# Attention and feed-forward on one core: transposes between second-product matmuls, a Prelu leaky step and a new schedule

## The chip, the cores and the metric

The kernel runs on one core of one Trainium2 chip. The metric is the device time of one execution in microseconds (us). The kernel before took 1224.76 us, the median of three runs (1224.69 to 1225.83).

## What is computed

Attention over 8 batches of 8 heads, 576 tokens of 64 numbers each, with a causal mask in blocks of 64 tokens; then a feed-forward part with a leaky step over all 4608 tokens:

```python
scores = np.where(block_i >= block_j, 0.125 * q @ k.T, -1e9)      # blocks of 64 tokens
attn = exp(scores - max); attn /= sum + 1e-9
x = (attn @ v), heads side by side                                 # 4608 x 512
h = x @ w_in                                                       # 512 -> 2048
out = np.maximum(0.01 * h, h) @ w_out                              # 2048 -> 512
```

All is float32. The weights come as 64-bit floats and are turned into float32 on the chip.

## The kernel before, in words

**Products in two halves.** Most products use the faster 32-bit format (fp32r). A float32 operand is split into a high part, a rounded copy, and a low part, the rest (`gh` and `gl`, `xh` and `xl`, `kh` and `kl`, `pth` and `ptl`), and a product is the sum of two or three matmuls. In batch 0 the scores of some heads and all values are plain float32 matmuls (L408, L539).

**Work.** The attention of batch 0 is done in two passes, `lo` (the first 320 tokens) and `hi` (the other 256) of each of its 8 heads; the 56 heads of batches 1 to 7 are `full`. A full head has five tiles of rows: tile 0 with 64 rows, tiles 1 to 4 with 128, each as wide as its mask allows (64, 192, 320, 448 and 576 columns). Its steps: scale and split q and k (L196 to L206, L393); scores of tiles 3, 0, 1, 2 into the two banks `p_s`, later of tile 4 (L411); mask (L420), row maximum (L427), exponential and row sum (L436), reciprocal (L450, L451) and normalising (L464 to L466, by GpSimd, VectorE or ScalarE); 15 transposes in groups of 4, 4, 5 and 2 into the two banks `p_t` (L487); the copies `pth` and `ptl`; 10 matmuls with the values (L542); the sums into `xr` (L528, L564).

**Feed-forward.** The tokens go in 18 chunks of 256. A chunk has 8 units of 256 of the 2048 inner columns. A unit has two runs of 12 matmuls of 256 columns into `p_h` (L630, the first product), then the leaky step into `g`: 0.01 h by ScalarE (or VectorE), from PSUM, and a maximum on VectorE, also from PSUM (L637). Then come `gh` and `gl`, and two runs of 6 matmuls of 512 columns into `p_o` (L648, the second product).

**Weights.** 64 pieces are loaded and converted by shifts and masks on VectorE (L319, L323); every other piece takes its sign by a third VectorE instruction (L328), the rest by a ScalarE sign (L332) and a GpSimd product (L333).

**Order.** No engine's order is written by hand. Each step is given to `Plan` with its buffers, an engine (or several to choose from), a price in ns, and a rank; a list schedule over the five engines then takes, on each engine that is free, the ready step of the lowest rank, and the instructions are issued in that order. The ranks come from the constants at the top of the file (RL to AHEAD). `HOLD` is how much longer a second choice of engine must wait than the first. Matmuls are priced at `max(109, n / 2.4 + 2.5)`, transposes at 109. While nothing else is ready early on, PE repeats a fill matmul (L701).

Of the kernel before, what the change touches and what calls it, by code (L numbers as in the profile page):

```python
# [32 lines left out]
# Ranks of the steps, in heads: inputs, preparation, wide tile, transposes, values, sums into x, normalising.  # L33
RL = 2.876
RP = 0.212
RB = 0.6
RT = 1.102
RV = 1.747
RX = 1.545
RN = -0.217  # L40
# Ranks of the feed-forward part and of the weights.
LEAD = 1.791
LAG = 1.995
RS = 1.48
RG = -0.41
OFF1 = 6
SL1 = 12.747
AHEAD = 0.041
# DMA latency; the fills that keep TensorE's clock up until the feed-forward part starts.
LAT = 1550  # L50
FILL = 235
FILLTO = 12


class Plan:
# [3 lines left out]
    HOLD = 816.955  # L59
# [14 lines left out]
    def add(self, choices, rank, reads=(), writes=(), lag=0):  # L74
        i = len(self.ops)
        deps = set()
        for k in reads:
            if k in self.writer:
                deps.add(self.writer[k])
        for k in writes:  # L80
            if k in self.writer:
                deps.add(self.writer[k])
            deps.update(self.readers.get(k, ()))
        for k in reads:
            self.readers.setdefault(k, []).append(i)
        for k in writes:
            self.writer[k] = i
            self.readers[k] = []
        deps.discard(i)
        self.ops.append((choices, rank, deps, lag))  # L90

    def run(self):
        n = total = len(self.ops)
        left = [len(o[2]) for o in self.ops]
        after = [[] for _ in range(n)]
# [3 lines left out]
        ends = [None] * n  # L99
# [3 lines left out]
        order, now, moved = [], 0, 0  # L103

        def offer(i):
            for k, (e, _, _) in enumerate(self.ops[i][0]):
                at = max([0] + [ends[d][1] + self.SYNC.get((ends[d][0], e), 0) for d in self.ops[i][2]])
                heapq.heappush(waiting, (at + k * self.HOLD, i, k))

        for i in range(n):  # L110
            if not left[i]:
                offer(i)
        while len(order) < n:
            while waiting and waiting[0][0] <= now:
                _, i, k = heapq.heappop(waiting)
                heapq.heappush(ready[self.ops[i][0][k][0]], (self.ops[i][1], i, k))
            for e, q in ready.items():
                while q and ends[q[0][1]]:
                    heapq.heappop(q)
                if q and free[e] <= now:  # L120
                    _, i, k = heapq.heappop(q)
                    choices, _, _, lag = self.ops[i]
                    _, cost, fn = choices[k]
                    if e == "PE" and now < 8000:
                        cost *= 2
                    free[e] = now + cost
                    if lag:
                        moved = max(moved, free[e] + 650) + lag
                    ends[i] = (e, moved + LAT if lag else free[e])
                    order.append(fn)  # L130
                    for j in after[i]:
                        left[j] -= 1
                        if not left[j]:
                            offer(j)
            if self.fill and free["PE"] <= now and now > self.fill[2]:
                if any(self.ops[i][0][0][0] == "PE" and self.ops[i][1] < self.fill[3] and not ends[i] for i in range(total)):
                    order.append(self.fill[1])
                    free["PE"] = now + self.fill[0] * (1 if now > 8000 else 2)
                    n += 1
                else:  # L140
                    self.fill = None
            times = [free[e] for e, q in ready.items() if (q or (e == "PE" and self.fill)) and free[e] > now]
            if waiting:
                times.append(waiting[0][0])
            if len(order) < n:
                now = max(now, min(times))
        for fn in order:
            fn()


def mm(n):
    return max(109, n / 2.4 + 2.5)


def product(n, plain):
    return max(109, n / 0.6) if plain else 2 * mm(n)
# [14 lines left out]
def pool2(n):  # L171
    return n * 2.35 + 25


def pool1(n):
    return n * 0.83 + 245
# [3 lines left out]
def attention_ffn(ctx: ExitStack, tc: tile.TileContext, qk: bass.AP, v: bass.AP, w_in: bass.AP, w_out: bass.AP, out: bass.AP):  # L180
# [13 lines left out]
    def copying(n, dst, src, sb=True, by=None, first="ACT", fast=True):  # L194
# [6 lines left out]
        both = [("ACT", act(n, sb), one), ("DVE", dve(n, sb and fast), two)]  # L201
        return both if first == "ACT" else both[::-1]

    def subtracting(n, dst, one, two, first="DVE"):
        both = [
            ("DVE", dve(n), lambda: nc.vector.tensor_sub(dst(), one(), two())),  # L206
# [26 lines left out]
    def rows(y, pool):  # L233
        prow[y] = [fixed([P, pw[t]], F32, f"prow{y}_{t}", None, pool) for t in range(NT)]
        for t in range(NT):
            nc.gpsimd.memset(prow[y][t][:, 0:BLK] if t == 0 else prow[y][t][:, kw[t] : pw[t]], 0.0)
# [45 lines left out]
    def weight_piece(num, rank, f, out_side, c0):  # L282
# [28 lines left out]
        if src.dtype != F32:  # L311

            def load():
# [5 lines left out]
                [("DVE", dve(w, True), lambda: nc.vector.tensor_single_scalar(bits(), bits(), 3, op=ALU.logical_shift_left))],  # L319
# [3 lines left out]
                [("DVE", dve(w), lambda: nc.vector.scalar_tensor_tensor(  # L323
# [3 lines left out]
            if num % SIGNS:  # L327
                add([("DVE", dve(w), lambda: nc.vector.scalar_tensor_tensor(  # L328
# [14 lines left out]
    def attention(i):  # L343
# [44 lines left out]
        else:  # L388
# [4 lines left out]
                [("DVE", dve(qe - qa), lambda: nc.vector.scalar_tensor_tensor(  # L393
# [10 lines left out]
        def scores(tiles):  # L404
            for t, ap, k0, k1 in tiles:
                cols = slice(q0[t], q0[t] + qn[t])
                if plain_s:
                    nc.tensor.matmul(ap, qkt[:rows, 0, cols], qkt[:rows, 1, k0:k1], start=True, stop=True)  # L408
                    continue
                for c, kk in enumerate((kh[z], kl[z])):  # L410
                    nc.tensor.matmul(ap, qs[z][:, cols], kk[:, k0:k1], start=c == 0, stop=c == 1)  # L411

        def softmax(tiles, mms, masks, r):
            banks = sorted({(sk, bk) for _, _, bk in tiles for bk in bk})
            cost = sum(product(k1 - k0, plain_s) for _, _, k0, k1 in mms)
            add([("PE", cost, lambda: scores(mms))], r, qkd, banks)
# [7 lines left out]
            for t, ap, bk in tiles:  # L424
# [3 lines left out]
                        nm[z][: qn[t], t : t + 1], ap, axis=AX.X if flat else AX.XY, op=ALU.max, negate=True  # L428
# [3 lines left out]
            def exponent(t, ap, flat):  # L432
                o = row(t, qn[t], pc[t], kw[t])
                if not flat:
                    o = o.rearrange("p (a k) -> p a k", a=2)
                nc.scalar.activation(  # L436
                    o, ap, AF.Exp, bias=nm[z][: qn[t], t : t + 1], scale=1.0, accum_out=sums[z][: qn[t], t : t + 1]
# [19 lines left out]
        def normalising(t, rr):  # L457
            by = rec[z][:rr, t : t + 1]

            def p():  # L460
# [4 lines left out]
                ("DVE", dve(kw[t], True), lambda: nc.vector.tensor_scalar_mul(p(), p(), by)),  # L465
# [4 lines left out]
        tiles = [(t, scored(k)[: qn[t], c : c + kw[t]], (k,)) for t, k, c in lay]  # L470
        softmax(
            tiles, [(t, ap, 0, kw[t]) for t, ap, _ in tiles],
            [ap[0:64, kw[t] - 64 : kw[t]] for t, ap, _ in tiles if t], r0,
        )
        if kind != "lo":
            softmax(
                [(4, p_s[:, :, 0:288], (0, 1))],
                [(4, p_s[:, 0, 0:288], 0, 288), (4, p_s[:, 1, 0:288], 288, 576)],
                [p_s[0:64, 1, 224:288]], r0 + RB,
            )  # L480
        for base, c0, w, items in tgroups[kind]:
            x = bank()

            def transposes(x=x, items=items):
                for t, j, c in items:
                    r = qn[t]
                    nc.tensor.transpose(p_t[x][:, c : c + r], row(t, r, j * P, P), ident[:r, :r])  # L487

            add([("PE", 109 * len(items), transposes)], r0 + RT, [k for t in sorted({a for a, _, _ in items}) for k in pkeys(t)], [("t", x)])
# [7 lines left out]
            def lo(base=base, w=w):  # L497
# [4 lines left out]
                subtracting(w, lo, lambda src=src: src, lambda hi=hi: hi)[:1],  # L502
# [34 lines left out]
        def passes(dst, j, cols, start, stop):  # L537
            if plain_v:
                nc.tensor.matmul(dst[0:64], vf[z][:, j], ptf[:, cols], start=start, stop=stop)  # L539
                return  # L540
            for k, pp in enumerate((pth, later["ptl"])):
                nc.tensor.matmul(dst, vs[z][:, j, :], pp[:, cols], start=start and k == 0, stop=stop and k == 1)  # L542

        def outer():
            c, w = ends[kind]
            passes(p_t[x0][:, :w], 0, slice(c, c + w), True, True)

        def values():
            last = spans[kind][-1][0]
            for j, a, e, c in spans[kind]:  # L550
                passes(p_t[x1][:, c : c + e - a], j, slice(a, e), j == 1, j == last)

        if kind in ends:
            add([("PE", product(ends[kind][1], plain_v), outer)], rv, ptd + [vkey], [("t", x0)])
        cost = sum(product(e - a, plain_v) for _, a, e, _ in spans[kind])
        add([("PE", cost, values)], rv, ptd + [vkey], [("t", x1)])
# [13 lines left out]
    def bank():  # L570
# [7 lines left out]
    }  # L578
    tgroups = {
# [16 lines left out]
        "full": [(1, 0, 512, 0), (2, 512, 960, 64), (3, 960, 1280, 192), (4, 1408, 1600, 320)],  # L596
# [23 lines left out]
    def ffn1(c, u, rank):  # L620
# [3 lines left out]
        for i in range(2):  # L624
            f = 2 * u + i

            def go(i=i, f=f):
                terms = [(w, x, d) for d in range(ND) for w, x in ((wih, xh), (wih, xl), (wil, xh))]
                for k, (w, x, d) in enumerate(terms):
                    nc.tensor.matmul(  # L630
                        hh[:, i, :], w[:, d, f * P : (f + 1) * P], x[:, d, :], start=k == 0, stop=k == len(terms) - 1
                    )
# [99 lines left out]
```

## Time and profile before

One execution was profiled; the span from its first to its last instruction is 1226.6 us, 1.84 us above the median of the three runs.

| engine | busy, us | share of the span |
|---|---|---|
| PE (matmuls) | 1188.9 | 97% |
| PEld (weight loads, beside PE) | 1056.9 | 86% |
| DVE (VectorE) | 785.2 | 64% |
| ACT (ScalarE) | 655.1 | 53% |
| POOL (GpSimd) | 476.0 | 39% |

A line of a group names the source line, the engine, the operation, what is written from what, the shapes and the count; then busy us and mean ns, and the idle time in front of it with what ended it. A line of the timeline begins with the start and the duration. A matmul's duration contains its way through the pipeline, so neighbouring matmuls overlap, and what one costs is read from the distance of starts.

### The profile page before, as it was taken

To read this page: it belongs to the slowest core of one execution; us is meant where nothing else is said; L and a number is where in the kernel's file an instruction comes from. 1 tells how busy PE (TensorE), PEld (TensorE's weight loads), DVE (VectorE), ACT (ScalarE), POOL (GpSimd) and SP (SyncE) were. 2 spreads that over 40 slices of the span, in tenths; PEclk is the share of its full clock that TensorE was granted. 3 is DMA by queue.
4 is the path that set the end of the run, shared out by engine and by line. 5 is a ranking of instruction groups with operands and counts; after the bars stand their busy time and mean duration, and the time that the engine had idled before them with its cause. 6 is when DMAs were issued, how large, how long until landed. Compare 5 with 4: busy or idle time off the path is not lost.

```text
span 1226.6 us, 21217 instructions
## 1 busy us (share of the span) xinstructions
PE 1188.9 (97%) x7718; PEld 1056.9 (86%) x7718; DVE 785.2 (64%) x1904; ACT 655.1 (53%) x1635; POOL 476.0 (39%) x569
## 2 busy tenths in 40 slices
PE   8888889899999999999999999999999999999998
PEld 6676678789999999999899999999999999999997
DVE  7989999888766767664454566767676766421110
ACT  6767755556555555554455455555555655422221
POOL 5687753334433334333333333433333333222222
PEclk9889999999999999999999999999999999999999
DMA  5555421221111211111111021112111110000000
GB/s 169 180 161 174 164 73 55 70 63 61 48 68 50 68 50 68 50 45 49 43 50 43 25 68 50 67 51 68 50 66 39 56 50 20 10 18 1 18 18 18
DMA packets 40233, 76.44 MB, mean 62 GB/s; under 512 B 4032, under 2 KB 23360, under 8 KB 40128
## 3 DMA queue, kind: packets, MB, share of 16 engines
q1 hardware_dynamic: 40128, 75.09, 19.1%
q8 instruction: 60, 0.98, 0.3%
q14 instruction: 45, 0.37, 0.1%
HBM read 65.63 MB, written 9.44 MB: 61 GB/s over the span
## 4 chain that ended last, share of the span: by engine, by line
PE 80%; DVE 14%; issue 2%; ACT 1%; DMA 1%; POOL 0%; SPq 0%; DVEq 0%; ACTq 0%; POOLq 0%
PE p_h L630 30%; PE p_o L648 29%; PE p_t L487 8%; PE p_t L542 6%; PE p_s L411 6%; DVE prow L465 2%; DVE val L323 2%; DVE nm L427 2%; DVE val L319 1%; DVE qs L393 1%; DVE val L328 1%; DVE kl L206 1%; DVE ptl L206 1%; DVE g L637 1%; DVE p_s L420 0%
## 5 line engine op out<-in xcount | busy, mean ns | idle before, releaser
L207 POOL TENSOR_TENSOR gl<-g,gh 128x512 fp32r<-128x512 f32 x143 | 187.3, 1310 | 383.5 <-ACT gh L196 363.7
L630 PE MATMUL p_h<-xh,wih 128*128 128x256 f32 x1152 | 333.8, 290 | 0.0
L630 PE MATMUL p_h<-xl,wih 128*128 128x256 f32 x1152 | 323.1, 280 | 0.0
L630 PE MATMUL p_h<-xh,wil 128*128 128x256 f32 x1152 | 322.7, 280 | 0.1
L464 POOL TENSOR_SCALAR prow<-prow,rec 128x192 f32<-128x192 f32 (+4 forms) x246 | 138.6, 575 | 298.6 <-DVE rec L451 226.7
L637 DVE TENSOR_TENSOR g<-p_h,g 128x512 f32<-128x512 f32 x144 | 99.4, 690 | 211.7 <-ACT g L199 211.2
L630 PEld LDWEIGHTS p_h<-xl,wih 128*128 128x128 f32 x1152 | 220.3, 191 | 3.3
L630 PEld LDWEIGHTS p_h<-xh,wih 128*128 128x128 f32 x1152 | 219.1, 190 | 3.6
L630 PEld LDWEIGHTS p_h<-xh,wil 128*128 128x128 f32 x1152 | 218.7, 190 | 0.3 <-POOL wil L207 0.3
L199 ACT ACTIVATE g<-p_h 128x512 f32<-128x512 f32 x137 | 81.9, 598 | 224.3 <-PE p_h L630 219.8
L436 ACT ACTIVATE prow<-p_s,nm 128x192 f32<-128x192 f32 (+4 forms) x308 | 160.0, 525 | 62.0 <-DVE nm L427 60.6
L648 PE MATMUL p_o<-woh,gh 128*128 128x512 f32 x576 | 181.7, 397 | 0.0
L648 PE MATMUL p_o<-wol,gh 128*128 128x512 f32 x576 | 180.3, 394 | 0.0
L648 PE MATMUL p_o<-woh,gl 128*128 128x512 f32 x576 | 180.0, 394 | 0.0
L487 PE MATMUL p_t<-ident,prow 128*128 128x128 f32 (+1 forms) x960 | 151.5, 284 | 13.5 <-POOL prow L464 8.0
L196 ACT CAST gh<-g 128x512 fp32r<-128x512 f32 x144 | 89.3, 620 | 134.8 <-PE p_o L648 68.1
L487 PEld LDWEIGHTS p_t<-ident,prow 128*128 128x128 f32 (+1 forms) x960 | 115.0, 143 | 42.2 <-issue 10.9
L196 ACT CAST pth<-p_t 128x448 fp32r<-128x448 f32 (+1 forms) x219 | 98.2, 496 | 80.6 <-PE p_t L487 78.3
L427 DVE TENSOR_REDUCE nm<-p_s 128x1 f32<-128x192 f32 (+4 forms) x308 | 135.4, 483 | 3.2
L206 DVE TENSOR_TENSOR ptl<-p_t,pth 128x512 fp32r<-128x512 f32 (+1 forms) x224 | 117.7, 562 | 20.9 <-ACT pth L196 20.5
L648 PEld LDWEIGHTS p_o<-woh,gl 128*128 128x128 f32 x576 | 108.8, 189 | 24.6
L648 PEld LDWEIGHTS p_o<-wol,gh 128*128 128x128 f32 x576 | 108.6, 189 | 23.9
(78 smaller groups left out, 1737.1 us busy)
## 6 DMA issues: line engine op xcount, KB each, us to landing
qk_in<-in_qk SPq DMA_DIRECT2D x56, 576.0 KB, 3.7
v_stage<-in_v SPq DMA_DIRECT2D x56, 160.0 KB, 2.7
out<-ob SPq DMA_DIRECT2D x35, 256.0 KB, 2.0
raw<-in_w_in SPq DMA_DIRECT2D x32, 256.0 KB, 3.0
raw<-in_w_out SPq DMA_DIRECT2D x32, 256.0 KB, 3.3
qk_in<-in_qk SPq DMA_DIRECT2D x6, 288.0 KB, 3.7
qk_in<-in_qk SPq DMA_DIRECT2D x8, 160.0 KB, 3.1
vf<-in_v SPq DMA_DIRECT2D x8, 160.0 KB, 3.3
```

Source lines behind the costliest of these rows:

```text
L196: one = lambda: nc.scalar.copy(dst(), src())
L199: one = lambda: nc.scalar.activation(dst(), src(), AF.Copy, scale=by)
L206: ("DVE", dve(n), lambda: nc.vector.tensor_sub(dst(), one(), two())),
L207: ("POOL", pool2(n), lambda: nc.gpsimd.tensor_sub(dst(), one(), two())),
L411: nc.tensor.matmul(ap, qs[z][:, cols], kk[:, k0:k1], start=c == 0, stop=c == 1)
L427: [("DVE", dve(kw[t]), lambda t=t, ap=ap, flat=flat: nc.vector.tensor_reduce(nm[z][: qn[t], t : t + 1], ap, axis=AX.X if flat else AX.XY, ...
L436: nc.scalar.activation(o, ap, AF.Exp, bias=nm[z][: qn[t], t : t + 1], scale=1.0, accum_out=sums[z][: qn[t], t : t + 1])
L464: ("POOL", pool1(kw[t]), lambda: nc.gpsimd.tensor_scalar(p(), p(), by, 1.0, op0=ALU.mult, op1=ALU.mult)),
L487: nc.tensor.transpose(p_t[x][:, c : c + r], row(t, r, j * P, P), ident[:r, :r])
L630: nc.tensor.matmul(hh[:, i, :], w[:, d, f * P : (f + 1) * P], x[:, d, :], start=k == 0, stop=k == len(terms) - 1)
L637: add([("DVE", dve(512), lambda: nc.vector.tensor_max(g, hh, g))], rank, [("h", z)], ["g"])
L648: nc.tensor.matmul(p_o[m], a[:, i, m * P : (m + 1) * P], w[:, 2 * u + i, :], start=u == 0 and k == 0, stop=u == NU - 1 and k == 5,)
```

## The change

- **Transposes dealt out.** `Plan` holds matmuls one by one. A group of transposes has the kind "short", a run of second-product matmuls the kind "long". When one of each is ready, their matmuls are issued in turn: long, short, long, short. A short step that is first in rank waits up to `PATIENCE` (424.6 ns) for a long one while PE has other work.
- **A new price of PE.** A matmul streams at `RATE` = 0.4414 ns a column; weight loads follow each other after at least 108 ns, and not before the matmul ahead has started; a matmul may start 57 ns after its load.
- **DVE and POOL.** VectorE's steps with both operands in SBUF (the name "DVE+") are not planned at the same time as a GpSimd step. GpSimd's prices are revised.
- **Matmul orders.** The wide scores go 448, 64, 448, 64, 320, 192, 320, 192 columns instead of both halves of one tile after each other. In full heads tile 0 is scored and transposed with 128 rows (its other rows aren't used further), its transpose moves from the third group to the fourth, and the value matmuls alternate wide and narrow.
- **Leaky step.** One ScalarE instruction, Prelu with alpha 0.01, from PSUM to `g`; VectorE's maximum is gone.
- **Constants.** HS 2 to 7 (heads of `hi` with plain float32 scores), SIGNS 2 to 3 (two of three signs by VectorE), HOLD 817 to 567, and all ranks.

The core of the diff:

```diff
-HS = 2
-SIGNS = 2
+HS = 7
+SIGNS = 3
...
+        def multiply(matmuls):
+            nonlocal load, start, stream
+            for cost, fn in matmuls:
+                if now < SLOW:
+                    cost *= 2
+                load = max(load + LOAD, start, now - 57)
+                start = max(start + stream, load + 57, now)
+                stream = cost
+                order.append(fn)
+            return start + stream
...
+                    if kind in ("short", "long") and short and long_:
+                        a = [(c, f, short[1]) for c, f in self.ops[short[1]][0][0][1]]
+                        b = [(c, f, long_[1]) for c, f in self.ops[long_[1]][0][0][1]]
+                        mixed = []
+                        while a or b:
+                            if b:
+                                mixed.append(b.pop(0))
+                            if a:
+                                mixed.append(a.pop(0))
...
-            for t, ap, k0, k1 in tiles:
-                cols = slice(q0[t], q0[t] + qn[t])
+            for y, (b, (t, ap, k0, k1, c)) in enumerate(tiles):
+                first, last = b not in banks[:y], b not in banks[y + 1 :]
+                cols = slice(q0[t], q0[t] + P)
...
-                for t, j, c in items:
-                    r = qn[t]
-                    nc.tensor.transpose(p_t[x][:, c : c + r], row(t, r, j * P, P), ident[:r, :r])
+            def transpose(t, j, c, x=x):
+                n = P if kind == "full" else qn[t]
+                return RATE * n, lambda: nc.tensor.transpose(p_t[x][:, c : c + n], row(t, n, j * P, P), ident[:n, :n])
...
-            (960, 64, 448, [(4, 4, 320), (2, 2, 0), (3, 2, 128), (4, 2, 256), (0, 0, 448)]),
-            (1408, 64, 192, [(3, 3, 0), (4, 3, 128)]),
+            (960, 64, 384, [(4, 4, 320), (2, 2, 0), (3, 2, 128), (4, 2, 256)]),
+            (1344, 64, 256, [(3, 3, 0), (4, 3, 128), (0, 0, 256)]),
...
-        add(copying(512, lambda: g, lambda: hh, sb=False, by=0.01), rank, [("h", z)], ["g"])
-        add([("DVE", dve(512), lambda: nc.vector.tensor_max(g, hh, g))], rank, [("h", z)], ["g"])
+        add([("ACT", act(512), lambda: nc.scalar.activation(g, hh, AF.Prelu, alpha=0.01))], rank, [("h", z)], ["g"])
```

More of the change, by code (lines that the diff above doesn't have):

```diff
@@ L32 @@
 VALS = 6
[L34 to L48, printed above, removed]
+RL = 7.153
+RP = 0.885
+RB = 0.516
+RT = 1.485
+RV = 1.932
+RX = -0.113
+RN = -0.908
+LEAD = 1.751
+LAG = 1.627
+RS = 0.514
+RG = -0.26
+OFF1 = 4.574
+SL1 = 11.938
+AHEAD = -0.663
 LAT = 1550
+HOLD = 567.499
+PATIENCE = 424.599
 FILL = 235
 FILLTO = 12
+LOAD = 108
+RATE = 0.4414
+SLOW = 8000
 class Plan:
-    HOLD = 816.955
     SYNC = {
@@ L102, in run, with end, best @@
         free = dict.fromkeys(ready, 0)
-        order, now, moved = [], 0, 0
+        port = {"DVE": 0, "POOL": 0}
+        order, now, moved, done = [], 0, 0, 0
+        load, start, stream = -LOAD, 0, 0
         def offer(i):
-            for k, (e, _, _) in enumerate(self.ops[i][0]):
+            for k, choice in enumerate(self.ops[i][0]):
+                e = choice[0]
+                e = e[:3] if e == "DVE+" else e
                 at = max([0] + [ends[d][1] + self.SYNC.get((ends[d][0], e), 0) for d in self.ops[i][2]])
-                heapq.heappush(waiting, (at + k * self.HOLD, i, k))
-        for i in range(n):
+                heapq.heappush(waiting, (at + k * HOLD, i, k))
+        def end(i, e, t):
+            nonlocal done
+            ends[i] = (e, t)
+            done += 1
+            for j in after[i]:
+                left[j] -= 1
+                if not left[j]:
+                    offer(j)
+        def multiply(matmuls):
[8 more added lines that the diff above has]
+            return start + stream
+        def best(kind):
+            found = [x for x in ready["PE"] if self.ops[x[1]][4] == kind and not ends[x[1]]]
+            return min(found) if found else None
+        for i in range(total):
             if not left[i]:
                 offer(i)
-        while len(order) < n:
+        while done < total:
             while waiting and waiting[0][0] <= now:
-                _, i, k = heapq.heappop(waiting)
-                heapq.heappush(ready[self.ops[i][0][k][0]], (self.ops[i][1], i, k))
+                at, i, k = heapq.heappop(waiting)
+                e = self.ops[i][0][k][0]
+                since[i] = at
+                heapq.heappush(ready["DVE" if e == "DVE+" else e], (self.ops[i][1], i, k))
+            wake = []
             for e, q in ready.items():
@@ L119, in run @@
                     heapq.heappop(q)
[L120 to L134, printed above, removed]
+                if not q or free[e] > now:
+                    continue
@@ new lines, in run @@
+                other = {"DVE": "POOL", "POOL": "DVE"}.get(e)
+                if other:
+                    open_ = port[other] <= now
+                    can = [x for x in q if not ends[x[1]] and (open_ or (e == "DVE" and self.ops[x[1]][0][x[2]][0] == "DVE"))]
+                    if not can:
+                        wake.append(port[other])
+                        continue
+                    x = min(can)
+                    q.remove(x)
+                    heapq.heapify(q)
+                elif e == "PE":
+                    live = [x for x in q if not ends[x[1]]]
+                    x = min(live)
+                    short, long_ = best("short"), best("long")
+                    if self.ops[x[1]][4] == "short" and not long_:
+                        other_ = [y for y in live if self.ops[y[1]][4] != "short"]
+                        if other_ and now < since[x[1]] + PATIENCE:
+                            x = min(other_)
+                    kind = self.ops[x[1]][4]
+                    if kind == "long":
+                        self.fill = None
+                    if kind in ("short", "long") and short and long_:
[7 more added lines that the diff above has]
+                                mixed.append(a.pop(0))
+                        at = {}
+                        for c, f, i in mixed:
+                            at[i] = multiply([(c, f)])
+                        free[e] = start + stream
+                        for y in (short, long_):
+                            q.remove(y)
+                            end(y[1], e, at[y[1]])
+                        heapq.heapify(q)
+                        continue
+                    q.remove(x)
+                    heapq.heapify(q)
+                    free[e] = multiply(self.ops[x[1]][0][x[2]][1])
+                    end(x[1], e, free[e])
+                    continue
+                else:
+                    x = heapq.heappop(q)
@@ L135, in run @@
+                _, i, k = x
+                choices, _, _, lag, _ = self.ops[i]
+                name, cost, fn = choices[k]
+                free[e] = now + cost
+                if name in ("DVE+", "POOL"):
+                    port[e] = free[e]
+                if lag:
+                    moved = max(moved, free[e] + 650) + lag
+                order.append(fn)
+                end(i, e, moved + LAT if lag else free[e])
             if self.fill and free["PE"] <= now and now > self.fill[2]:
@@ L137, in run @@
                     order.append(self.fill[1])
-                    free["PE"] = now + self.fill[0] * (1 if now > 8000 else 2)
-                    n += 1
+                    free["PE"] = now + self.fill[0] * (1 if now > SLOW else 2)
+                    start, stream = now, free["PE"] - now
                 else:
                     self.fill = None
-            times = [free[e] for e, q in ready.items() if (q or (e == "PE" and self.fill)) and free[e] > now]
+            times = wake + [free[e] for e, q in ready.items() if (q or (e == "PE" and self.fill)) and free[e] > now]
             if waiting:
                 times.append(waiting[0][0])
-            if len(order) < n:
-                now = max(now, min(times))
+            if done < total:
+                now = max(now + 1e-6, min(times))
+        self.span = max(t for _, t in ends)
         for fn in order:
             fn()
[L151 to L156, printed above, removed]
 def dve(n, fast=False):
@@ L535, in attention, with product @@
             x0 = x1
-        def passes(dst, j, cols, start, stop):
+        def product(dst, j, cols, half, start, stop, split=False):
             if plain_v:
[L539 to L544, printed above, removed]
-            c, w = ends[kind]
-            passes(p_t[x0][:, :w], 0, slice(c, c + w), True, True)
@@ L548, in values @@
[L548 to L556, printed above, removed]
+                go = lambda: nc.tensor.matmul(dst[0:64], vf[z][:, j], ptf[:, cols], start=start, stop=stop)
@@ new lines, in product, with go @@
+                return 4 * RATE * (cols.stop - cols.start), go
+            def go():
+                src, to = (pth, later["ptl"])[half], dst
+                if split:
+                    src = src[:, 1088:1600].rearrange("p (a b) -> p a b", a=2)[:, :, 192:256]
+                    to = dst.rearrange("p (a b) -> p a b", a=2)
+                else:
+                    src = src[:, cols]
+                nc.tensor.matmul(to, vs[z][:, j, :], src, start=start, stop=stop)
+            return RATE * (cols.stop - cols.start), go
@@ new lines, in attention @@
+        halves = (0,) if plain_v else (0, 1)
+        last = 3 if kind == "full" else spans[kind][-1][0]
+        values = [[
+            product(p_t[x1][:, c : c + e - a], j, slice(a, e), y, j == 1 and y == 0, j == last and y == halves[-1])
+            for y in halves
+        ] for j, a, e, c in spans[kind]]
+        if kind in ends:
+            c, w = ends[kind]
+            outer = [product(p_t[x0][:, :w], 0, slice(c, c + w), y, y == 0, y == halves[-1], kind == "full") for y in halves]
+            if kind == "full":
+                one, two, three, four = values
+                values = [[y for x in zip(one + two, outer + four) for y in x], three]
+                add([("PE", values[0][:4])], rv, ptd + [vkey], [("t", x0), ("t", x1)])
+                values[0] = values[0][4:]
+            else:
+                add([("PE", outer)], rv, ptd + [vkey], [("t", x0)])
@@ L578, in attention_ffn @@
     }
+    turns = {
+        "full": ((3, 0), (0, 0), (3, 1), (0, 1), (2, 0), (1, 0), (2, 1), (1, 1)),
+        "hi": ((3, 0), (3, 1)),
+    }
     tgroups = {
```

108 lines of the change are left out of this document (59 added, 49 removed).

## The prediction

> **What bounds the kernel now.** I read the page first, then the busy times by stretch, the chain of waits of the first stretch, the groups by line and form, and last the start times of single matmuls.
>
> ```profile
> span 1226.6 us, 21217 instructions
> PE 1188.9 (97%) x7718; PEld 1056.9 (86%) x7718; DVE 785.2 (64%) x1904; ACT 655.1 (53%) x1635; POOL 476.0 (39%) x569
> ```
>
> ```profile
> 0.00:277.00 277.00, 243.06 (x1405) 198.64 (x1406) 250.82 (x610) 174.62 (x482) 156.01 (x199) 0.93 0.40 123
> 277.00:1085.00 808.00, 808.00 (x5426) 733.57 (x5425) 512.39 (x1266) 446.29 (x1096) 287.67 (x346) 1.00 0.15 50
> 1085.00:1226.60 141.60, 137.87 (x890) 124.67 (x889) 21.94 (x31) 34.20 (x57) 32.31 (x25) 1.00 0.04 16
> ```
>
> The second fence gives, for each stretch, its length and then the busy time of PE, weight loads, DVE, ACT and POOL; the last columns are granted clock, DMA share and GB/s. From 277 to 1085 us PE is never idle (808.00 of 808.00) at full clock: there only a matmul that costs less PE time helps, and a DVE instruction less is worth nothing. In the first 277 us PE is idle for 33.9 us, its clock is 0.93, and DVE is the busiest engine (250.8). The last stretch has 3.7 us of idle.
>
> **What a matmul costs PE.** The middle of the run asks for one price: what a transpose between two longer matmuls takes. Two rows of the chain of waits give the plain rates, rows of the timeline the mixed ones (start, duration, what; a duration includes the pipeline, so only differences of starts count).
>
> ```profile
> 1211.88 2.75 PE p_h L630 x24
> 1214.63 8.26 PE p_o L648 x36
> ```
>
> ```profile
> 720.87 0.19 PEld L648 LDWEIGHTS p_o<-woh,gh 128*128 128x128 f32 x1
> ```
>
> ```profile
> 720.87 0.63 PE L648 MATMUL p_o<-woh,gh 128*128 128x512 f32 x2
> ```
>
> ```profile
> 701.64 0.22 PE L542 MATMUL p_t<-pth,vs 128*128 128x128 f32 x1
> 701.70 0.27 PE L542 MATMUL p_t<-ptl,vs 128*128 128x128 f32 x1
> 701.81 0.45 PE L542 MATMUL p_t<-pth,vs 128*128 128x512 f32 x1
> 702.09 0.39 PE L542 MATMUL p_t<-ptl,vs 128*128 128x512 f32 x1
> 702.33 0.36 PE L542 MATMUL p_t<-pth,vs 128*128 128x448 f32 x1
> ```
>
> ```profile
> 294.31 0.37 PE L411 MATMUL p_s<-kh,qs 128*128 128x448 f32 x1
> ...
> 295.41 1.04 PE L487 MATMUL p_t<-ident,prow 128*128 128x128 f32 x8
> ...
> 296.40 0.28 PE L630 MATMUL p_h<-xl,wih 128*128 128x256 f32 x1
> ```
>
> ```profile
> 299.10 1.17 PE L487 MATMUL p_t<-ident,prow 128*128 128x128 f32 x7
> ...
> 300.23 0.28 PE L630 MATMUL p_h<-xl,wih 128*128 128x256 f32 x1
> ```
>
> A 512-column matmul takes 8.26/36 = 0.229 us, a 256-column one 2.75/24 = 0.115 us, so 0.448 ns a column; 128 columns would stream in 0.057 us. Eight transposes and one 256-column matmul take 296.40 - 295.41 = 0.99 us, which leaves (0.99 - 0.115)/8 = 0.109 us for a transpose. What fills those 0.109 us is the next weight load: the load row at 720.87 starts when the matmul before the loaded one starts, so PE loads one set ahead and no more. I read the rule as: a matmul costs PE the longer of its own stream and the load of the next weights (0.109 us).
>
> The alternative stands in the new planner: a matmul may start 57 ns after its load begins. The value rows decide. There two short matmuls (128 columns) precede two long ones. By my rule the stretch from 701.64 to 702.33 is 2 x 0.109 + 2 x 0.229 = 0.68 us; by the planner's (second short after 0.057, the next load begins at 0.108, the first long at 0.165) it is 0.165 + 0.458 = 0.62. Measured: 0.69. The recorded start of the first 512-column matmul (701.81) does come early, but the time is given back before the next (0.28 instead of 0.229). The Trainium skill, page "TensorE: Matmul & The Clock Gate", section on the array as 16 sub-arrays of 32×32, says the opposite: a matmul can begin before its weight load completes. By that, dealing would gain; the trace shows such early starts and no gain from them.
>
> **The change, part by part.** First a count: the wide tile's maximum runs once a head (8 of the second pass over batch 0, 56 full ones), and the middle stretch has 47 of them, all full heads of 15 transposes.
>
> ```profile
> L427 DVE TENSOR_REDUCE nm<-p_s 128x1 f32<-128x576 f32 x47 | 35.4, 753 | 1.2
> ```
>
> *Transposes dealt out between second-product matmuls.* One transpose between two 512-column matmuls: its load hides in the first one's 0.229, but the load of the second can begin only as the transpose starts, 0.109 again. A pair costs 0.338 us mixed or apart: gain 0. Bounds: nothing at the one end, 0.052 us for each of about 705 transposes (47 heads of 15) behind 277 us at the other, 37 us. I take 0, because the value rows lie at that end. A transpose now stands in front of second-product matmuls in PE's in-order queue; one whose rows aren't normalised yet holds them up. In the middle stretch PE is the late engine, so I cost it at nothing; the price without that cover is in the rivals.
>
> *The first tile's transpose padded to 128x128.* The group at 299.10 holds one 64x64 transpose among seven. To 300.23 it takes 1.13 us; without the 256-column matmul and six transposes 1.13 - 0.115 - 0.654 = 0.36 us are left for that one, against 0.109. Padded, it saves 0.25 us less rounding; I take 0.24. About 47 of 56 heads lie behind 277 us: -11.3 us, all on the path. The other nine fall where PE has idle time; I count nothing.
>
> *Score order, and its first tile padded.* The eight wide score matmuls take 295.41 - 294.31 = 1.10 us. After: two of 448 (0.201 each), two of 320 (0.143), and the four short ones at a full load each (0.109), 1.12 us. Before, two loads were of 64 columns and shorter. Loss 0.02 to 0.04, so +1.5 us over 47 heads. The value matmuls change order alone, and the longer of stream and load stays the same for each: 0.
>
> *Prelu, and less for DVE early on.* These rows are of the first 277 us.
>
> ```profile
> L637 DVE TENSOR_TENSOR g<-p_h,g 128x512 f32<-128x512 f32 x17 | 11.6, 681 | 0.2
> L200 DVE TENSOR_SCALAR g<-p_h 128x512 f32<-128x512 f32 x7 | 4.8, 685 | 1.2 <-PE p_h L630 1.2
> L393 DVE SCALAR_TENSOR_TENSOR qs<-qk_in,qs 64x256 fp32r<-64x256 f32 x6 | 5.4, 894 | 0.2
> L206 DVE TENSOR_TENSOR kl<-qk_in,kh 128x576 fp32r<-128x576 f32 x10 | 11.0, 1095 | 0.2
> L328 DVE SCALAR_TENSOR_TENSOR val<-raw,val 128x256 int32<-128x256 int32 x32 | 15.2, 473 | 0.0
> L465 DVE TENSOR_SCALAR prow<-prow,rec 128x192 f32<-128x192 f32 (+3 forms) x31 | 30.7, 1012 | 0.1
> ```
>
> Prelu takes the maximum (11.6) and the seven scalings that DVE had (4.8) off DVE; on ACT it takes the scaling's place, at the same size. HS = 7 leaves the splitting out for five more heads: 5 x (0.894 + 1.095) = 9.9 us off DVE. SIGNS = 3 sends 42 instead of 32 signs by DVE: +10 x 0.473 = 4.7. Net -21.6 us. HS also gives PE two more passes over 5 x 1024 score columns, 5 x 2 x 1024 x 0.448 ns = 4.6 us, hidden by the 33.9 us of idle; without that it would count whole. Behind 277 us the 0.69 us of each maximum is worth nothing.
>
> *New prices and ranks; DVE and POOL kept apart.* DVE's normalisation is where the old plan goes wrong:
>
> ```profile
> 195.87 3.22 DVE L465 TENSOR_SCALAR prow<-prow,rec 128x192 f32<-128x192 f32 x2
> ```
>
> ```profile
> 196.23 1.29 POOL L207 TENSOR_TENSOR gl<-g,gh 128x512 fp32r<-128x512 f32 x1
> 197.47 1.43 POOL L207 TENSOR_TENSOR kl<-qk_in,kh 128x576 fp32r<-128x576 f32 x1
> ```
>
> ```profile
> L465 DVE TENSOR_SCALAR prow<-prow,rec 128x320 f32<-128x320 f32 x39 | 18.4, 472 | 0.0
> ```
>
> Two of them last 3.22 us, just until POOL's two subtractions are over (198.90). In the middle stretch the 320-wide one takes 0.472 us (last row), early the mean of all is 1.012 (fence before): 31 x 0.54 = 16.7 us are lost to this. The new plan treats the two engines as sharing a port for these forms, which could avoid part of it.
>
> ```profile
> by line: issue 10.4%; DVE prow L465 9.8%; DVE val L323 9.0%; DVE nm L427 8.8%; DVE val L319 6.2%; PE p_h L630 5.0%; PE p_t L487 3.6%; DVE qs L393 3.5%; DVE val L328 3.3%; DVE kl L206 3.2%; PE p_o L648 3.0%; DVE ptl L206 2.9%; DVE g L637 2.6
> ```
>
> On the chain of the first 277 us the DVE lines listed sum to 49%. So half of the 21.6 us (10.8) and, by the same half, half of the 16.7 if half is avoided (4.2) should come off: -15 us. Bounds: 0, and 33.9, the whole of PE's idle. That the new ranks lose time there is a rival below. The tail holds 3.7 us; the leaky step isn't last there: 0.
>
> **Sum.** -11.3 + 1.5 - 15 = -24.8 us. The profiled span of 1226.6 us becomes 1201.8; the median of the runs, 1224.76, lies 1.84 under that span, so the forecast is 1200.0.
>
> **Rivals.**
>
> *Dealing pays.* PE really starts at half a load, as the planner has it: 37 us more, 1163. For it: recorded starts 0.06 us after a short matmul. Against it: 0.69 us, not 0.62, in the value rows.
>
> *A dealt transpose waits (slower).* A transpose that comes before its normalised rows stalls the second-product matmuls queued behind it. Early on this wait exists:
>
> ```profile
> PE p_t L487 <- POOL prow L464: 8.0, 8, 2.1
> ```
>
> 8.0 us in 8 times, 1.0 us each. Once a head behind 277 us is +47 us: 1247. It decides from 24.8/47 = 0.53 us a head. For it: a plan that prices PE too low by 0.05 us a transpose issues things in an order that PE doesn't keep. Against it: PE then runs late, and the others are ready earlier than planned.
>
> *Prelu reloads ScalarE's table.*
>
> ```profile
> L199 ACT ACT_TABLE_LOAD x1 | 1.3, 1283 | 0.7 <-PEq L725 0.7
> ```
>
> One load serves everything now. If Prelu and the exponential needed different ones, each of the 144 Prelus (18 chunks of 8 units) would bring up to two, 2.57 us. In the first 277 us that is 17 x 2.57 = 44 us on the softmax's path: 1244 or more. Against it: copies, signs and exponentials share one load. The Trainium skill ("ScalarE: Activation LUTs", "What ACT_TABLE_LOAD costs") adds a drain of 1.38 us to each switch, which no row here shows; its section on table sets doesn't list Prelu with the exponential. With that drain two switches of 2.66 us for each of the 127 Prelus behind 277 us would put 676 us on top of ACT's 446 + 34 in 950 us, 207 too many: an estimate of some 1400 from that page.
>
> *The refit gives it back.* The new ranks cost the first stretch some 10 us instead of saving 15: 1225. The trace of before has nothing on them.
>
> **How the numbers follow.** The forecast has 0.64; its own range is 1181 (all 33.9 us of idle gone) to 1215 (none). Dealing pays: 0.13; waiting transposes: 0.12; table reloads: 0.05; given back: 0.06. The range runs from 1158, a little under the second case, to 1227, over the last; it leaves out the two slower cases (0.17) and the far end of "dealing pays". Within 0.2% (2.4 us, about what a measurement of this kernel can tell from no change) lies most of "given back": 0.05. Faster: 0.77. Slower: 0.18.
>
> **What would show it.** Right: second-product matmul to transpose to second-product matmul repeats every 0.34 us; seven-transpose groups lose their 0.36 us member; PE stays full behind the first stretch, which ends some 15 us earlier with fewer 3-us normalisations. Wrong: a repeat near 0.286 us (dealing pays), idle PE before L487's successor in the middle (waits), more than one table load, or a first stretch as long as before.

## The result, and the profile after

The changed kernel takes 1193.48 us (median of four runs, 1190.43 to 1194.49) against 1225.3 us beside it: a ratio of 0.9736, 95% interval 0.9718 to 0.9754. The forecast was 1200.0, in a range from 1158 to 1227. The profiled execution's span is 1192.3 us.

Page of the changed kernel:

```profile
span 1192.3 us, 21079 instructions
PE 1175.5 (99%) x7778; PEld 1041.4 (87%) x7778; DVE 680.2 (57%) x1782; ACT 657.4 (55%) x1652; POOL 431.5 (36%) x505
```

PE is idle for 16.8 us instead of 37.7. The same 277 us of the run as in the prediction's second fence, and the chain of waits over them:

```profile
0.00:277.00 277.00, 264.06 (x1632) 221.86 (x1633) 221.91 (x655) 205.00 (x562) 100.85 (x135) 0.98 0.41 125
```

```profile
by line: PE p_h L734 17.8%; PE p_o L753 17.7%; PE p_t L573 10.1%; PE p_t L625 8.0%; PE p_s L488 7.7%; PE p_o L806 7.3%; PE p_s L494 6.5%; PE p_t L635 6.1%; DVE nm L512 2.9%; PE p_h L488 2.1%; DVE ptl L284 1.3%; issue 1.3%; DVE prow L550 1.2
```

PE's busy time rose from 243.06 to 264.06 us and the granted clock from 0.93 to 0.98; VectorE fell from 250.82 to 221.91, GpSimd from 156.01 to 100.85, and ScalarE rose from 174.62 to 205.00. (It is the same time, not the same work: the changed kernel is further on at 277 us.) Before, VectorE's lines made up half of this chain; now the PE lines shown sum to 83%, of which 7.3 (L806) are the fill matmul.

To see where the time went I take two marks on PE, the first matmul of the first product in the fourth and in the sixteenth chunk. Timeline of before (two queries), then of after:

```profile
334.71 0.30 PE L630 MATMUL p_h<-xh,wih 128*128 128x256 f32 x1
...
1086.66 0.28 PE L630 MATMUL p_h<-xh,wih 128*128 128x256 f32 x1
```

```profile
309.02 0.28 PE L734 MATMUL p_h<-xh,wih 128*128 128x256 f32 x1
...
1053.73 0.28 PE L734 MATMUL p_h<-xh,wih 128*128 128x256 f32 x1
```

Up to the fourth chunk 334.71 - 309.02 = 25.7 us are gone. The twelve chunks of the middle take 744.71 us instead of 751.95, 7.2 less. The rest, 138.6 instead of 139.9, gives 1.4; it holds 300 second-product matmuls instead of 306, and six of 0.229 us are 1.4, so this part is moved, not saved. Together 34.3 us, the difference of the two spans.

The stretch up to the fourth chunk, before and after, then the fill matmuls alone, before and after (all of them lie in the first 100 us; busy time of PE and of weight loads):

```profile
0.00:334.71 334.71, 300.77 (x1796) 250.79 (x1796) 295.39 (x723) 211.44 (x574) 179.05 (x226) 0.94 0.36 112
0.00:309.02 309.02, 296.08 (x1851) 250.57 (x1852) 243.00 (x704) 222.32 (x606) 114.96 (x152) 0.98 0.39 117
```

```profile
0.00:100.00 100.00, 16.43 (x102) 14.76 (x102) 0.91 0.56 170
0.00:100.00 100.00, 24.22 (x162) 22.58 (x162) 1.00 0.60 177
```

PE's idle time there falls from 33.9 to 12.9 us, but the fill, which PE repeats while it waits, grows from 16.4 to 24.2. So PE waits 13.2 us less (37.2 instead of 50.4). The other 12.5 of the 25.7 us are PE's own work, which takes 271.9 us instead of 284.3, at a granted clock of 0.98 instead of 0.94.

### The profile page after: what moved, and what is told of

It reads as the page before. It is cut to its first block, busy times and chain, and to the rows that moved or that the text cites. A ratio compares the mean times of both kernels' runs of the same rounds, so it can differ in the third digit from the quotient of the medians.

```text
span 1192.3 us, 21079 instructions
## 1 busy us (share of the span) xinstructions
PE 1175.5 (99%) x7778; PEld 1041.4 (87%) x7778; DVE 680.2 (57%) x1782; ACT 657.4 (55%) x1652; POOL 431.5 (36%) x505
## 4 chain that ended last, share of the span: by engine, by line
PE 96%; DVE 2%; ACT 1%; DMA 0%; issue 0%; ACTq 0%; DVEq 0%
PE p_o L753 33%; PE p_h L734 33%; PE p_t L573 9%; PE p_t L635 8%; PE p_s L494 8%; PE p_t L625 2%; PE p_s L488 2%; PE p_o L806 2%; DVE nm L512 1%; PE p_h L488 0%; DVE ptl L284 0%; DVE prow L550 0%; DMA qk_in<-in_qk 0%; ACT prow L521 0%; DMA raw<-in_w_in 0%
## 5 line engine op out<-in xcount | busy, mean ns | idle before, releaser
L573 PE MATMUL p_t<-ident,prow 128*128 128x128 f32 x960 | 239.7, 274 | 3.1 <-DVE ptl L284 0.9
L753 PE MATMUL p_o<-wol,gh 128*128 128x512 f32 x576 | 219.9, 453 | 0.0
L753 PE MATMUL p_o<-woh,gh 128*128 128x512 f32 x576 | 204.0, 426 | 0.0
L753 PE MATMUL p_o<-woh,gl 128*128 128x512 f32 x576 | 192.2, 415 | 0.0
L549 POOL TENSOR_SCALAR prow<-prow,rec 128x192 f32<-128x192 f32 (+4 forms) x214 | 119.1, 568 | 167.1 <-DVE rec L536 124.3
L614 DVE TENSOR_TENSOR xr<-p_t,xr 64x64 f32<-64x64 f32 x112 | 50.4, 450 | 164.6 <-ACT xr L274 164.3
L573 PEld LDWEIGHTS p_t<-ident,prow 128*128 128x128 f32 x960 | 130.2, 141 | 13.9 <-DVE ptl L284 1.9
L753 PEld LDWEIGHTS p_o<-woh,gh 128*128 128x128 f32 x576 | 105.5, 189 | 28.1 <-issue 2.6
L274 ACT CAST pth<-p_t 128x384 fp32r<-128x384 f32 (+3 forms) x175 | 81.5, 469 | 63.9 <-PE p_t L573 59.5
L753 PEld LDWEIGHTS p_o<-woh,gl 128*128 128x128 f32 x576 | 96.6, 189 | 20.0
```

The lines of the kernel that those rows point to most:

```text
L274: one = lambda: nc.scalar.copy(dst(), src())
L549: ("POOL", pool1(kw[t]), lambda: nc.gpsimd.tensor_scalar(p(), p(), by, 1.0, op0=ALU.mult, op1=ALU.mult)),
L573: return RATE * n, lambda: nc.tensor.transpose(p_t[x][:, c : c + n], row(t, n, j * P, P), ident[:n, :n])
L753: nc.tensor.matmul(p_o[m], a[:, i, m * P : (m + 1) * P], w[:, 2 * u + i, :], start=u == 0 and k == 0, stop=u == NU - 1 and k == 5,)
```

## The experiments

The runs fall into three groups of four, each on one chip with runs of the kernel before beside it (medians 1225.23, 1227.3 and 1226.32 us). Ratios are to those, over all runs, so they aren't exactly the quotients of the medians; the changed kernel's is 0.9736.

### Dealing out taken back

```diff
-                        free[e] = start + stream
+                        order[-len(mixed) :], free[e] = [f for s in (short, long_) for _, f, i in mixed if i == s[1]], start + stream
```

> The changed kernel with its plan and its other engines untouched, but where a group of transposes and a run of second-product matmuls were dealt out, the transposes are now issued first and the run behind them. If a matmul costs the longer of its stream and the next weight load, dealing is worth nothing: 1193 us, at most 3 off, and a chunk in the middle takes 64.0 us as now. If a matmul may start at half a load, as the planner has it, each of some 800 dealt transposes loses 0.052 us: +40, 1233.

Measured: 1192.38 us, ratio 0.9732 (0.9716 to 0.9749): no difference. Between the two marks it takes 744.14 us (307.58 to 1051.72), 0.6 less than dealt out. The timelines show why there is no gain. First the changed kernel, dealt out:

```profile
703.82 0.39 PE L753 MATMUL p_o<-woh,gh 128*128 128x512 f32 x1
704.05 0.27 PE L573 MATMUL p_t<-ident,prow 128*128 128x128 f32 x1
704.08 0.48 PE L753 MATMUL p_o<-woh,gh 128*128 128x512 f32 x1
704.39 0.27 PE L573 MATMUL p_t<-ident,prow 128*128 128x128 f32 x1
```

then the run with the transposes in front:

```profile
701.71 0.60 PE L573 MATMUL p_t<-ident,prow 128*128 128x128 f32 x4
702.06 0.70 PE L753 MATMUL p_o<-woh,gh 128*128 128x512 f32 x2
702.60 0.62 PE L753 MATMUL p_o<-wol,gh 128*128 128x512 f32 x2
```

Transpose to transpose with one 512-column matmul between is 704.39 - 704.05 = 0.34 us, as forecast (0.338; the planner's price says 0.286). The long matmul behind a transpose has a recorded start 0.03 us after it, but the next instruction starts only 0.31 us after that. Apart, four transposes and two long matmuls take 702.60 - 701.71 = 0.89 us, again 4 x 0.109 + 2 x 0.229. The Trainium skill, "TensorE: Matmul & The Clock Gate", in the section on the array as 16 sub-arrays, lets a matmul begin before its weight load completes. With the weights of 128 columns used here the trace shows an early recorded start and no time gained.

### The padded transpose taken back

```diff
-                n = P if kind == "full" else qn[t]
-                return RATE * n, ...
+                n = qn[t]
+                return RATE * (P if kind == "full" else n), ...
```

> The changed kernel with only the first tile's transpose of a full head back at 64x64; plan and order are the same. If the 64-row transpose costs 0.24 us more on PE wherever it stands: 56 heads, +13, 1206 to 1207. If dealing hides it between long matmuls: no change, 1193.

Measured: 1209.01 us, ratio 0.9866 (0.9848 to 0.9885): 15.5 us slower. The small transpose in its timeline:

```profile
700.23 0.27 PE L573 MATMUL p_t<-ident,prow 128*128 128x128 f32 x1
700.26 0.48 PE L753 MATMUL p_o<-wol,gh 128*128 128x512 f32 x1
700.67 0.27 PE L573 MATMUL p_t<-ident,prow 64*128 64x64 f32 x1
700.87 0.50 PE L753 MATMUL p_o<-wol,gh 128*128 128x512 f32 x1
701.22 0.39 PE L753 MATMUL p_o<-woh,gl 128*128 128x512 f32 x1
```

From the full transpose ahead of it to the second long matmul behind it, two dealt pairs, pass 701.22 - 700.23 = 0.99 us; two pairs of full size take 2 x 0.34 = 0.68. Here the small transpose costs 0.31 us more. Between the marks (310.10 and 1068.33 us) the run loses 13.5 us over 652 transposes, 43.5 heads of 15: again 0.31 each. The 15.5 us of the medians over 56 heads are 0.28 each. It is a smaller transpose, dearer on PE.

### The score order taken back

```diff
-                first, last = b not in banks[:y], b not in banks[y + 1 :]
-                cols = slice(q0[t], q0[t] + P)
+                first, last = (c == 0, c == 1) if kind == "full" else ...
+                cols, ap = (slice(q0[t], q0[t] + qn[t]), ap[: qn[t]]) if kind == "full" else ...
...
-            add([("PE", list(scores(mms)))], r, qkd, banks)
+            add([("PE", [(x[0], y[1]) for x, y in zip(scores(mms), scores(sorted(mms, ...)))])], r, qkd, banks)
```

The last line keeps the plan's prices and issues the matmuls in the order 3, 0, 1, 2, both halves of a tile together.

> The changed kernel with the wide scores of full heads in the order of before (both halves of a tile after each other, tile 0 with 64 columns of weights); plan and other engines the same. By the longer of stream and load the old order is 0.02 to 0.04 us a head cheaper: 1 to 2 us faster, 1191 to 1192.5. By the planner's price, where alternating hides loads, it is some 0.15 us a head dearer: +8, 1202.

Measured: 1189.01 us, ratio 0.9704 (0.9687 to 0.9721), a median 4.5 us lower; the intervals overlap by 0.0003. Timeline of the changed kernel and of this run, from the first wide score to the first product's second matmul:

```profile
698.08 0.40 PE L494 MATMUL p_s<-kh,qs 128*128 128x448 f32 x2
698.32 0.48 PE L494 MATMUL p_s<-kl,qs 128*128 128x448 f32 x2
...
699.20 0.31 PE L734 MATMUL p_h<-xh,wih 128*128 128x256 f32 x1
699.34 0.28 PE L734 MATMUL p_h<-xl,wih 128*128 128x256 f32 x1
```

```profile
694.69 0.37 PE L494 MATMUL p_s<-kh,qs 128*128 128x448 f32 x1
...
695.77 0.28 PE L734 MATMUL p_h<-xh,wih 128*128 128x256 f32 x1
695.89 0.28 PE L734 MATMUL p_h<-xl,wih 128*128 128x256 f32 x1
```

1.26 us with alternating widths, 1.20 in the old order: 0.06 us a head, 3.4 over 56. Between the marks (307.33 and 1048.90 us) this run takes 741.57 us, 3.1 less. This part of the change costs time.

### The two-step leaky step put back

```diff
-        add([("ACT", act(512), lambda: nc.scalar.activation(g, hh, AF.Prelu, alpha=0.01))], rank, [("h", z)], ["g"])
+        add(copying(512, lambda: g, lambda: hh, sb=False, by=0.01), rank, [("h", z)], ["g"])
+        add([("DVE", dve(512), lambda: nc.vector.tensor_max(g, hh, g))], rank, [("h", z)], ["g"])
```

> The changed kernel with the leaky step of before: a scaling by ScalarE or VectorE and a maximum on VectorE, in the new plan. If a VectorE instruction counts only in the first stretch: 16.4 us more VectorE there, half of it on the path, +8, 1201, and a chunk in the middle still takes 64.0 us. If the step's length sets the pace everywhere: 0.69 us for each of 144, up to +99.

Measured: 1200.2 us, ratio 0.9797 (0.9779 to 0.9815): 6.7 slower, near the 8 expected and far from 99. Prelu takes what the scaling took, and no table is reloaded (a group of before, then two of the changed kernel):

```profile
L199 ACT ACTIVATE g<-p_h 128x512 f32<-128x512 f32 x137 | 81.9, 598 | 224.3 <-PE p_h L630 219.8
```

```profile
L741 ACT ACTIVATE g<-p_h 128x512 f32<-128x512 f32 x144 | 85.7, 595 | 234.4 <-PE p_h L734 234.1
L277 ACT ACT_TABLE_LOAD x1 | 1.3, 1283 | 0.7 <-PEq L830 0.7
```

By the same two marks on PE (312.66 and 1060.81 us) this run loses 3.6 us up to the fourth chunk and 3.4 in the middle. The middle part was not expected. 1.4 us of it are six more second-product matmuls in front of the second mark (1158, not 1152). PE is busy for all but 0.2 us there, so for the other 2 us some PE work got dearer in the other order. Which, was not tested.

### HS, SIGNS

`HS = 2` and, in another run, `SIGNS = 2`.

> The changed kernel with HS = 2 as before: five more heads of the second pass over batch 0 split q and k again. All of it lies in the first stretch. If VectorE sets the pace there by half: 9.9 us more VectorE, +5, less up to 4.6 us of PE passes saved, so 1194 to 1198. If PE is now the bound of the first stretch, the passes saved count whole: 1189.

> The changed kernel with SIGNS = 2 as before: ten signs go from VectorE back to ScalarE and GpSimd, 4.7 us less VectorE in the first stretch. If VectorE is still what the first stretch waits for: -2, 1191. If GpSimd and the port it shares are the scarcer: +2 to +5, 1196 to 1198.

Measured: 1196.26 us for HS, ratio 0.9784 (0.973 to 0.9839), and 1195.96 for SIGNS, ratio 0.9744 (0.9717 to 0.9772). One of HS's four runs took 1208.9 us, at a clock of 0.983, which widens its interval. Both intervals reach the changed kernel's: neither constant makes a difference that these runs can tell.

### The port rule taken out of the plan

```diff
-                if name in ("DVE+", "POOL"):
+                if False:
                     port[e] = free[e]
```

> The changed kernel whose plan no longer keeps VectorE's two-operand SBUF steps and GpSimd's steps apart; prices and ranks stay. If the forecast's term is right (half of the 16.7 us of slow normalisations avoided, half of that on the path): +4, 1197, and long VectorE normalisations return. If the rule is what made the first stretch 27 instead of 15 us shorter: +12 or more, 1205. If it does nothing: 1193.

Measured: 1215.81 us, ratio 0.9907 (0.9879 to 0.9936): some 21 us slower (0.0171 of 1225). The forecast's term for this rule, 4 us, was far too small. It looked at the normalisations alone, and they aren't what the rule shortens. VectorE's normalisations of the first 277 us, after and in this run:

```profile
L550 DVE TENSOR_SCALAR prow<-prow,rec 128x192 f32<-128x192 f32 (+4 forms) x33 | 14.0, 453 | 0.1
```

```profile
L550 DVE TENSOR_SCALAR prow<-prow,rec 64x64 f32<-64x64 f32 (+4 forms) x33 | 12.1, 392 | 0.3
```

Without the rule 33 of them take 12.1 us, with it 14.0, and before 31 took 30.7: the long ones of before didn't come back, although that had been expected. What shortened them, these runs don't show. Groups of the weights' two shifts, of before (L323, L319), after and this run:

```profile
L323 DVE SCALAR_TENSOR_TENSOR val<-raw,val 128x256 int32<-128x256 int32 x64 | 33.9, 546 | 0.1
L319 DVE TENSOR_SCALAR val<-val 128x256 int32<-128x256 int32 x64 | 30.4, 496 | 8.3 <-ACT val L199 8.2
```

```profile
L401 DVE SCALAR_TENSOR_TENSOR val<-raw,val 128x256 int32<-128x256 int32 x64 | 27.0, 434 | 0.0
L397 DVE TENSOR_SCALAR val<-val 128x256 int32<-128x256 int32 x64 | 19.9, 335 | 7.6 <-ACT val L277 7.6
```

```profile
L401 DVE SCALAR_TENSOR_TENSOR val<-raw,val 128x256 int32<-128x256 int32 x64 | 36.0, 573 | 0.1
L397 DVE TENSOR_SCALAR val<-val 128x256 int32<-128x256 int32 x64 | 28.0, 450 | 7.9 <-ACT val L277 7.9
```

Nothing in these instructions changed, and yet they take 546, 434 and 573 ns, and 496, 335 and 450. GpSimd's busy time up to 277 us is 156.0 before, 100.9 after and 153.4 in this run. That GpSimd's work is the cause still had to be shown.

### GpSimd kept busy for nothing

```diff
-                [("DVE+", dve(w), lambda: nc.vector.scalar_tensor_tensor(
+                [("DVE+", dve(w), lambda: ([nc.gpsimd.tensor_sub(pth[:, c : c + P], ident, ident) for c in (0, P)], nc.vector.scalar_tensor_tensor(
```

> The changed kernel with the same order on every engine, and 128 subtractions added on GpSimd (128x128, about 0.44 us each, one pair per weight piece, 56 us in all, in the first 140 us, where GpSimd is idle most of the time); they write a buffer that is not in use yet, and nobody needs their result. If GpSimd's work slows VectorE's (contention): the weight shifts (0.434 and 0.335 us now) go back towards the 0.55 and 0.50 of before, 64 x 0.25 = 16 us more VectorE, and the time rises by 8 to 16, 1201 to 1209. If only waiting for GpSimd's results costs time, an added subtraction delays one by 0.9 us at most where GpSimd is busy: up to +4, and the shifts keep their durations.

Measured: 1206.34 us, ratio 0.9825 (0.9802 to 0.9847): 11 us slower. Groups of the first 145 us of this run:

```profile
L401 POOL TENSOR_TENSOR pth<-ident 128x128 fp32r<-128x128 f32 x123 | 63.2, 541 | 0.0
```

```profile
L401 DVE SCALAR_TENSOR_TENSOR val<-raw,val 128x256 int32<-128x256 int32 x61 | 30.6, 514 | 0.0
L397 DVE TENSOR_SCALAR val<-val 128x256 int32<-128x256 int32 x61 | 25.8, 447 | 7.9 <-ACT val L277 7.9
...
L512 DVE TENSOR_REDUCE nm<-p_s 128x1 f32<-128x576 f32 x8 | 6.1, 758 | 0.3
```

and of the same 145 us of the changed kernel:

```profile
L512 DVE TENSOR_REDUCE nm<-p_s 128x1 f32<-128x576 f32 x9 | 6.8, 757 | 0.3
```

The changed kernel's 64 pairs of shifts all lie in these 145 us too (434 and 335 ns, shown above). Work that nobody waits for, with GpSimd busy for 106.7 us instead of 50.0, made the shifts 80 and 112 ns longer, while the row maximum, which reads PSUM alone, kept its 757 ns. So GpSimd's work slows these VectorE steps, whose operands lie in SBUF. Whether the maximum is spared as a reduction or because it reads PSUM, these runs don't separate. The Trainium skill, "SBUF — State Buffer", section "Who interferes with whom", has the rule: VectorE and GpSimd share a pair of ports, held for a whole instruction, and a reduction never contends. The trace agrees on the slower shifts and on the reduction (758 against 757 ns); that the pair is held for a whole instruction no experiment here tests.

### Old ranks

All ranks and HOLD of before in the changed kernel; then only the attention's (RL to RN); then only the others and HOLD.

> The changed kernel with the ranks and HOLD of before (RL to AHEAD), the rest as changed. The middle stays at 64.0 us a chunk. If the unforeseen 12 us of the first stretch come from the refitted ranks: +12, 1205. If the prices, the port rule and Prelu bring them whatever the ranks: 1193 to 1196.

> The changed kernel with the attention ranks of before (RL to RN), and the feed-forward and weight ranks and HOLD as changed. If what the refit brings (27 us with all ranks old) lies in the attention steps' order (inputs and splitting earlier, normalising later): +15 to +27, 1208 to 1220. If it lies in the other ranks: 1193 to 1198.

> The changed kernel with the feed-forward and weight ranks and HOLD of before, and the attention ranks as changed. If the refit's gain lies there: +15 to +27, 1208 to 1220. If in the attention ranks: 1193 to 1198. If any mixture of the two sets loses it, the gain is a matter of the set as a whole: both this and the run with old attention ranks above 1205.

Measured: 1220.04 us, ratio 0.9954 (0.993 to 0.9977), for all; 1205.79, ratio 0.9819 (0.979 to 0.9849), for the attention's; 1210.53, ratio 0.9862 (0.984 to 0.9883), for the others. Either half costs, 10 and 15 us, and both 27. The stretch up to the fourth chunk, with all ranks old (the profiled execution, 1226.2 us, is one of the longer of its ten):

```profile
0.00:340.00 340.00, 310.42 (x1816) 259.56 (x1817) 251.74 (x712) 220.29 (x597) 127.76 (x166) 0.92 0.35 107
```

The middle takes what it takes in the changed kernel, 744.8 us by the marks (339.70 and 1084.53). The loss lies in the first stretch, in PE's idle time (29.6 us, 12.9 after) and its lower clock (0.92, 0.98 after). With the old attention ranks alone, the marks (320.76 and 1066.95 us) put 1.5 us of the loss into the middle.

### The better parts together

The old score order of the full heads, and transposes in front of the long run.

> The changed kernel with the scores of full heads in the old order and 64 columns for tile 0 (as in the run that gave 1189.0) and the transposes issued ahead of the second-product run instead of dealt out (1192.4). If both act on PE alone they add up: 4.5 + 1.1 less, 1188. If dealing matters in company with the score order: 1189 or more.

Measured: 1188.93 us, ratio 0.9686 (0.9664 to 0.9707), below the changed kernel's interval. It is the fastest version; from the run with the score order alone it can't be told apart.

## Why the prediction was right, point by point

- **What a matmul costs.** Right: the longer of its stream and the next weight load. Dealing out is worth nothing, and the rival in which it pays falls: the repeat is 0.34 us, and undoing it changes nothing.
- **Padded transpose.** Right. Forecast 0.24 us a head; undone, 0.31 among dealt transposes, 15.5 us in all.
- **Score order.** Forecast a loss of 0.02 to 0.04 us a head; it is 0.06. Up to the first product the two orders take 1.12 and 1.08 us, the upper end of the forecast. The other 0.02 lie just behind, where the forecast stopped: after the narrow last score matmul the first product's second matmul starts 0.14 us after its first, after a wide one 0.12.
- **The middle.** It came out as -7.2 us against -9.8 forecast. Between the marks lie 43 heads (645 transposes before, 652 after), not the 47 of the forecast's longer stretch, so its two terms are -10.3 and +1.4 there. With the score order's measured 3.1 and the 0.6 that dealing costs, the sum there is -6.6; with 0.31 us for each padded transpose instead of 0.24 it would be -9.6. The measured -7.2 lies between; what padding is worth in the old order was not tested.
- **The first stretch.** VectorE, slowed by GpSimd, did hold PE back there, but the terms were wrong: -15 forecast, -25.7 measured, of which 13.2 us are PE's waiting and 12.5 its own work. The forecast had read the granted clock (0.93) and gave it no term. By the mean clocks PE lost an estimated (1 - 0.94) x 334.7 = 20 us of full-speed time up to the mark before and (1 - 0.98) x 309.0 = 6 after; what set the clock was not tested. So the forecast's bound, the 33.9 us of idle time, bounds only a part of what could be gained. The mis-sized terms are "-4.2" for the port rule and nothing for the ranks. Taking out the rule costs 21 us, old ranks 27, Prelu 7. These can't be added (they sum to 55): each one taken away brings back idle PE time in this stretch, 29.7, 29.6 and 16.1 us against 12.9. The port term failed in kind too, since it counted only normalisations, which stay short without the rule; the weights' shifts alone take 64 x (573 - 434 + 450 - 335) ns = 16.3 us more without it, and between before and after they got 64 x (546 - 434 + 496 - 335) ns = 17.5 us cheaper. That the waiting alone came out near the forecast's 15 us is luck.
- **HS and SIGNS.** The sum of 9.9 and -4.7 us of VectorE was neither confirmed nor refuted; no effect could be measured. For HS the forecast itself set 4.6 us of PE work against it.
- **Rivals.** No waiting transposes: PE is never idle in the middle (745.00 of 745.00 us between 309 and 1054). One table load as before. The refit gave nothing back: of the parts taken out one by one, none costs more than the new ranks. The time also lies in the forecast's own narrower range, 1181 to 1215.

## What to carry to other kernels

When PE is never idle, price a matmul by the longer of its own stream and the weight load of the next, and check any reordering against differences of starts two instructions on; a recorded start close behind a short matmul isn't a saving. Count filler work as waiting, and give the granted clock a term of its own. Before moving work from VectorE to GpSimd, look whether VectorE's unchanged instructions take longer while GpSimd runs. Where several engines wait for each other, parts of a change don't add up, and a plan's order can be worth as much as the instructions that it removes.

## What was not expected of the hardware

A 64x64 float32 transpose among dealt ones costs PE 0.31 us more than a 128x128 one, in a place where a full one costs 0.11. And in these runs the time repeats less well where the clock is lower: with all ranks old, ten runs spread from 1215.8 to 1229.1 us at mean clocks of 0.987 to 0.975, the longest at the lowest clock, where the best version's four lie within 1.6 us at 0.996 to 0.997.
